# Operand tiles moved to multiples of 128 bytes, and jobs moved between the cast and the low half in a chained fp32 kernel

## The chip, the core and the metric

The kernel runs on one core of a Trainium2 chip. The metric is the time of one execution on the device in microseconds (us): before the change 1062.71 us, the median of three runs from 1061.94 to 1063.3. TensorE (PE in the profile) multiplies, VectorE (DVE) and ScalarE (ACT) do the elementwise work, SyncE (SP) issues nearly all DMAs. [...]

## The reference

Three layers, one after the other, on 6016 tokens of 256 channels:

```python
qn = q / (norm(q, axis=1) + 1e-06);  kn = k / (norm(k, axis=1) + 1e-06)
s = kn.transpose(0, 2, 1) @ qn / tau          # 256 x 256: over channels, not tokens
a = exp(s - s.max(-1));  a /= a.sum(-1) + 1e-09
x = v @ a                                     # 6016 x 256
h = x @ w_in;   x = (h * sigmoid(1.702 h)) @ w_out        # 256 -> 2048 -> 256
h = x @ w2_in;  out = maximum(0.01 h, h) @ w2_out         # 256 -> 2048 -> 256
```

The four weight matrices arrive as float64 and the result is float32.

## The kernel before

**Products.** Every float32 operand x of the two large layers is split into a high part (x rounded to the format float32r) and a low part (the rest). A product is three matmuls (`terms`, L84): high by high, high weight by low token, low weight by high token. Tokens are the moving operand, 512 columns at a time (448 in the last pair of blocks); a weight block of 128 x 128 is the stationary one and is loaded for each matmul.

**Front.** q and k are streamed through `qk` tiles and multiplied in plain float32 (L365), the squares give the norms, and the softmax gives the 256 x 256 matrix, whose halves are `eth` and `etl`. `fold(f)` (L461) multiplies it into the first layer's input weights, so that v can be used as it is.

**Layers.** There are 8 weight groups f and 6 pairs of token blocks. In the first pair of the first layer `hidden_first` (L639) makes the hidden block directly; one call per f and half s, 16 calls, and `fold(f + 1)` between them. From the second pair on, `step` (L673) makes a 2 x 2 block of products with 7 instead of 8 multiplications (sums of token blocks in `xa` and `xb`, sums of weight blocks in `wa`). Results of the activation go to `gd`, `g11` and `g22` as halves and wait in the list `pend` until `emit_y` (L504) issues their second product into the banks y00 to y11. A step is 12 matmuls with `xa`, 12 with a waiting pair of halves, 9 with `xb`, and 12 again.

**Order.** All instructions are written out by hand in each engine's order; there is no scheduler. Preparing the weights (turning float64 words to float32, splitting, forming sums) is one long generator of small jobs, `jobs` (L272); `go_on(n)` puts the next n of them where it stands. A job is mostly one DVE instruction, sometimes an ACT instruction or a DMA. `fetch` does the same for the next pair's tokens. Before the last pair of the first layer the rest of the jobs is issued at once (L754). `switch` (L621) splits the next pair's `xb`.

**Places of the tiles.** Tiles of a pool stand one after the other, each rounded up to 32 bytes per partition. `ident` takes 512 bytes and `ones` 4, so 32; all that follows in the pool `early` begins 32 bytes past a multiple of 128: `wa` and `wo` of f = 0 to 2, `xa0`, `xb`, `eth`, `etl`. Then come `den` and `rden` with 8 bytes each, and all that follows them begins 96 bytes past such a multiple: `ws`, `qk`, and in the pool `late` `xa1`, `wa` and `wo` of f = 3 to 7, `g11`, `g22`, `gd`. The layer-2 weights take the same places as the layer-1 ones. All the sizes of these operands are multiples of 128 bytes.

Of the kernel before, what the change touches and what calls it, by code (L numbers as in the profile page):

```python
# [7 lines left out]
F32 = mybir.dt.float32  # L8
# [9 lines left out]
def tile_kernel(  # L18
# [28 lines left out]
    nc = tc.nc  # L47
# [24 lines left out]
    ps = ctx.enter_context(tc.tile_pool(name="ps", bufs=1, space=bass.MemoryType.PSUM))  # L72

    ident = const.tile([P, P], F32, name="ident")
    ones = const.tile([P, 1], F32, name="ones")
    x2 = [dram.tile([P, 4, w], F32, name=f"x2{p}") for p, w in enumerate(width)]
    w1raw = [dram.tile([P, 4, P], F32, name=f"w1raw{f}") for f in range(NF)]
    w2a = [dram.tile([P, 2, 7, P], F32, name=f"w2a{f}") for f in range(NF)]
# [31 lines left out]
    with tc.manual_schedule():  # L110
# [78 lines left out]
        def convert(key):  # L189


            name, f = key
            if key not in scaled:
                scale_words(raws[key])
                scaled.add(key)
            t = raws[key]
            b = t[:, :, :, 1]
            a = early.tile([P, 4, P], I32, tag="ta", name="ta", bufs=2)
            nc.vector.tensor_scalar(  # L199
                out=a, in0=t[:, :, :, 0], scalar1=29, scalar2=7,  # L200
                op0=ALU.logical_shift_right, op1=ALU.bitwise_and,
            )
            yield
            nc.vector.scalar_tensor_tensor(  # L204
                out=a, in0=b, scalar=-0x80000000, in1=a, op0=ALU.bitwise_and, op1=ALU.bitwise_or
            )
            yield
            nc.vector.scalar_tensor_tensor(  # L208
                out=a, in0=b, scalar=3, in1=a, op0=ALU.logical_shift_left, op1=ALU.bitwise_or
            )  # L210
            raws.pop(key)
            to_convert.remove(key)
            next_load()
            scale_next()
            yield
            a = a.bitcast(F32)
            flat = a.rearrange("p k c -> p (k c)")
            if name == "wo":
                hi, lo = (wo[f][:, s].rearrange("p k c -> p (k c)") for s in range(2))
                nc.vector.tensor_copy(hi, flat)  # L220
                yield
                subtract(lo, flat, hi.bitcast(F32))
                yield
                return
            if name == "wi":
                wi = early.tile([P, 2, BLK], F32R, tag="ws", name="wi", bufs=2)
                nc.vector.tensor_copy(wi[:, 0], flat)
                yield
                subtract(wi[:, 1], flat, wi[:, 0].bitcast(F32))
                ready[f] = wi  # L230
                yield
                return
            if name == "w2o":
                w = early.tile([P, 2, BLK], F32R, tag="ws", name="w2o", bufs=2)
                nc.scalar.copy(w[:, 0], flat)
                yield
                subtract(w[:, 1], flat, w[:, 0].bitcast(F32))
                nc.sync.dma_start(
                    out=w2o[f].rearrange("p h s c -> p h (s c)"), in_=w.bitcast(F32)
                )  # L240
                yield
                return
            hi, lo = (
                early.tile([P, 7, P], F32R, tag="ws", name=f"w2a{x}", bufs=2) for x in "hl"
            )
            nc.scalar.copy(hi[:, :3], a[:, :3])
            yield
            subtract(lo[:, :3], a[:, :3], hi[:, :3].bitcast(F32))
            yield
            yield from combine(a)  # L250
            nc.scalar.copy(hi[:, 3:], a)
            yield
            subtract(lo[:, 3:], a, hi[:, 3:].bitcast(F32))
            for i, x in enumerate((hi, lo)):
                nc.sync.dma_start(out=w2a[f][:, i], in_=x.bitcast(F32))
            yield

        ready, combined = {}, set()

        def combine_first(f):  # L260

            a = early.tile([P, 4, P], F32, tag="ta", name="ts", bufs=2)
            nc.sync.dma_start(out=a, in_=w1raw[f])
            yield
            yield from combine(a)
            nc.scalar.copy(wa[f][:, 0, 3:], a)
            yield
            subtract(wa[f][:, 1, 3:], a, wa[f][:, 0, 3:].bitcast(F32))
            combined.add(f)
            yield  # L270

        def jobs():  # L272
            for key in order[:2 * NF]:
                yield from convert(key)
            for f in range(NF):
                yield from combine_first(f)
            for key in order[2 * NF:]:
                yield from convert(key)
# [8 lines left out]
        big = [front.tile([P, 2, 2, 4, C], F32, name=f"qk{i}") for i in range(4)]  # L287
        acc = front.tile([P, 2, 2, C], F32, name="acc")
        sc = front.tile([P, KC, C], F32, name="sc")
        taub = front.tile([P, 1], F32, name="taub")  # L290
        rtau = front.tile([P, 1], F32, name="rtau")
        dq = front.tile([P, KC, P], F32, name="dq")
        root = front.tile([P, 4], F32, name="root")
        rr = front.tile([P, 4], F32, name="rr")
        rn = front.tile([P, 4], F32, name="rn")
        mx = front.tile([P, KC], F32, name="mx")
        rk = front.tile([P, KC], F32, name="rk")
        st = front.tile([P, KC, C], F32, name="st")
        den = early.tile([P, KC], F32, name="den")
        rden = early.tile([P, KC], F32, name="rden")  # L300
        nc.vector.memset(acc, 0.0)


# [157 lines left out]
        def fold(f):  # L461

            wi = ready.pop(f).rearrange("p h (d n) -> p h d n", d=KC)
            pw = bank("h2").rearrange("p (k n) -> p k n", k=KC)
            for kc in range(KC):
                c0 = slice(kc * P, (kc + 1) * P)
                for d in range(KC):
                    terms(pw[:, kc], (eth[:, d, c0], etl[:, d, c0]), (wi[:, 0, d], wi[:, 1, d]),
                          d == 0, d == KC - 1)
            raw = early.tile([P, 4, P], F32, tag="tp", name="raw")  # L470
            for kc in range(KC):

                nc.scalar.activation(
                    out=raw[:, 0::3] if kc == 0 else raw[:, 1:3],
                    in_=pw[:, kc].rearrange("p (s n) -> p s n", s=2), func=AF.Copy,
                    scale=rden[:, kc:kc + 1],
                )
            hi, lo = wa[f][:, 0, :4], wa[f][:, 1, :4]
            nc.vector.tensor_copy(hi, raw)  # L479
            subtract(lo, raw, hi.bitcast(F32))  # L480
            nc.sync.dma_start(out=w1raw[f], in_=raw)
# [145 lines left out]

        def reload(f):

            pool = early if f < EARLY else late  # L630
            wa[f] = pool.tile([P, 2, 7, P], F32R, tag=f"wa{f}", name=f"wa2{f}")
            nc.sync.dma_start(out=wa[f].bitcast(F32), in_=w2a[f])

        def reload_out(f):
            pool = early if f < EARLY else late
            wo[f] = pool.tile([P, 2, 2, C], F32R, tag=f"wo{f}", name=f"wo2{f}")
            nc.sync.dma_start(out=wo[f].bitcast(F32), in_=w2o[f])

        def hidden_first(f):  # L639
# [5 lines left out]
            for u in range(2):  # L645
# [2 lines left out]
                    terms(hp, (wa[g][:, 0, at[kc]], wa[g][:, 1, at[kc]]),  # L648
                          (x[:, 0, u], x[:, 1, u]), kc == 0, kc == KC - 1)
                act(1, h[:, u], hp)  # L650
            halves(gd[:, 0], gd[:, 1], h)
            for u in range(2):
                pend.append((1, 0, u, f, gd[:, 0, u], gd[:, 1, u]))

# [5 lines left out]
        for f in range(NF):  # L660
            for s in range(2):
                hidden_first(f + s * NF)

                if f + 1 < NF and s == (f == 0):
                    while f + 1 not in ready:
                        go_on(1)
                    fold(f + 1)
                if f + 1 < NF or s == 0:
                    emit_y(len(pend) - 2)
                go_on(6)  # L670
                fetch()

        def step(layer, p, f):  # L673
# [24 lines left out]
            g22 = late.tile([P, 2, BLK], F32R, tag="gs", name="g22", bufs=3)[:, :, :w]  # L698
            act(layer, tt, tt)
            nc.scalar.copy(g22[:, 0], tt)  # L700
            second = pend[2:]
            del pend[2:]
            emit_y(2)
            go_on(2)
            fetch()
            subtract(g22[:, 1], tt, g22[:, 0].bitcast(F32))
            product(pa, A12, xbt, B21, more=True)
# [9 lines left out]
            subtract(g11[:, 1], tp, g11[:, 0].bitcast(F32))  # L717
            act(layer, cc, cc)
            pend.extend(second)
            emit_y(2)  # L720
            pend.append((layer, p, 1, f + NF, g22[:, 0], g22[:, 1]))
            pend.append((layer, p, 0, f, g11[:, 0], g11[:, 1]))
            begun.append((layer, p, f, cc))
            go_on(3)
            fetch()

        begun = []
# [1 line left out]
        def finish_step():  # L729
            if begun:  # L730
# [4 lines left out]
                pend.append((layer, p, 1, f, gd[:, 0, 0], gd[:, 1, 0]))  # L735
                pend.append((layer, p, 0, f + NF, gd[:, 0, 1], gd[:, 1, 1]))

        steps = [(layer, p) for layer in (1, 2) for p in range(NPAIR)]
        for i, (layer, p) in enumerate(steps[1:], 1):
            switch(layer, p)  # L740
            coming[0] = prefetch(*steps[i + 1]) if i + 1 < len(steps) else iter(())
            for f in range(NF):
                while f not in combined:
# [5 lines left out]
                        reload_out(f - 1)  # L749
                elif i == NPAIR and f == 0:  # L750
                    reload_out(NF - 1)
            while coming[0] and next(coming[0], 1) != 1:
                pass
            if (layer, p) == (1, NPAIR - 2):  # L754
                for _ in work:
                    pass
        finish_step()
        emit_y(len(pend))

# [29 lines left out]
```

## Time and profile before

| what | value |
|---|---|
| median of three runs | 1062.71 us |
| the profiled execution's own time | 1062.7 us |
| its span in the profile | 1060.9 us |
| TensorE busy | 1041.6 us (98%), 4664 matmuls |
| VectorE busy | 777.7 us (73%) |
| ScalarE busy | 590.2 us (56%) |
| mean granted TensorE clock | 0.996 |

The chain of work that ended last is followed back from the last instruction; 93% of it is TensorE, 48% in `y` products and 44% in `h` products. Busy time of TensorE counts a matmul from its start to its modelled end, and these overlap: one of 512 columns is listed with some 390 ns while the next one starts some 230 ns after it. How fast matmuls follow each other is read from the chain, whose pieces run from one start to the next, or from the starts in the timeline.

### The profile page before, as it was taken

The numbers are of one execution on the slowest core, as the hardware profiler recorded it, in microseconds if no ns is written. First come the engines' busy times: TensorE is split into PE (matmuls) and PEld (weight loads), VectorE is DVE, ScalarE is ACT, GpSimd is POOL, SyncE is SP. The second block draws the span as 40 slices with busy tenths as digits, with TensorE's granted clock in tenths as the row PEclk, the third lists the DMA queues.
The fourth block names the chain that finished last, engine by engine and source line by source line (L and its number), as shares of the span: only waits on it lengthen the run. The fifth ranks groups of instructions, "written<-read, shape, count | busy, mean of one in ns | idle before, by whom it ended". The sixth has DMA issues, their size and how long they took to land.

```text
span 1060.9 us, 12596 instructions
## 1 busy us (share of the span) xinstructions
PE 1041.6 (98%) x4664; PEld 867.8 (82%) x4664; DVE 777.7 (73%) x1185; ACT 590.2 (56%) x862; POOL 0.7 (0%) x7
## 2 busy tenths in 40 slices
PE   7999999999999999999999999999999999999996
PEld 6878887888888888888998888888888888888996
DVE  5979868788888888887676667667577667667654
ACT  5555546566656656565556555555555555555452
POOL 0000000000000000000000000000000000000000
PEclk9999999999999999999999999999999999999998
DMA  9645323015224324202644002101200300300202
GB/s 357 247 109 140 125 84 90 11 38 157 95 75 125 89 76 149 74 36 86 212 164 149 1 1 43 38 1 25 55 0 15 66 1 1 74 1 1 41 1 35
DMA packets 120077, 81.82 MB, mean 77 GB/s; under 512 B 93392, under 2 KB 104400, under 8 KB 118736
## 3 DMA queue, kind: packets, MB, share of 16 engines
q1 hardware_dynamic: 116160, 80.43, 25.6%
q10 hardware_dynamic: 3856, 0.59, 0.4%
q8 instruction: 36, 0.59, 0.2%
q14 instruction: 25, 0.20, 0.1%
HBM read 55.05 MB, written 25.95 MB: 76 GB/s over the span
## 4 chain that ended last, share of the span: by engine, by line
PE 93%; DVE 3%; DMA 2%; ACT 1%; issue 0%; SPq 0%; DVEq 0%; ACTq 0%
PE y L88 48%; PE h L88 44%; DVE acc L95 2%; DMA qk<-in_k_dram 1%; DMA qk<-in_q_dram 1%; SPq L316 0%; DVE gd L92 0%; ACT gd L91 0%; DVE ta L208 0%; ACT sq L332 0%; DVE ta L204 0%; ACT h L496 0%; DVE xb L92 0%; DVE o L557 0%; DVE ta L199 0%
## 5 line engine op out<-in xcount | busy, mean ns | idle before, releaser
L88 PE MATMUL y<-gd,wo 128*128 128x512 f32 (+1 forms) x1248 | 297.7, 387 | 0.0
L88 PE MATMUL h<-xa,wa 128*128 128x512 f32 (+1 forms) x1152 | 279.5, 388 | 0.3 <-DVE wa L479 0.3
L88 PEld LDWEIGHTS y<-gd,wo 128*128 128x128 f32 x1248 | 233.8, 188 | 46.7
L88 PEld LDWEIGHTS h<-xa,wa 128*128 128x128 f32 x1152 | 216.0, 188 | 44.2 <-DVE wa L479 0.5
L88 PE MATMUL y<-g,wo 128*128 128x512 f32 (+1 forms) x1056 | 250.6, 386 | 0.0
L88 PEld LDWEIGHTS y<-g,wo 128*128 128x128 f32 x1056 | 198.3, 188 | 38.2
L88 PE MATMUL h<-xb,wa 128*128 128x512 f32 (+1 forms) x888 | 221.6, 389 | 2.0 <-ACT tp L689 1.0
L88 PEld LDWEIGHTS h<-xb,wa 128*128 128x128 f32 x888 | 166.2, 187 | 37.4 <-DVE tt L95 1.6
L95 DVE TENSOR_TENSOR tv<-tp,h 128x512 f32<-128x512 f32 (+1 forms) x88 | 59.4, 675 | 123.1 <-PE h L88 119.9
L95 DVE TENSOR_TENSOR cc<-tv,h 128x512 f32<-128x512 f32 (+1 forms) x176 | 116.5, 673 | 39.7 <-PE h L88 38.6
L689 ACT COPY tp<-h 128x512 f32<-128x512 f32 (+1 forms) x88 | 50.8, 577 | 102.3 <-PE h L88 100.5
L92 DVE TENSOR_TENSOR gd<-cc,gd 128x1024 fp32r<-128x1024 f32 (+1 forms) x88 | 105.1, 1194 | 1.5 <-ACT gd L91 1.5
L91 ACT CAST gd<-cc 128x1024 fp32r<-128x1024 f32 (+1 forms) x88 | 90.9, 1033 | 0.0
L498 ACT ACTIVATE cc<-cc 128x1024 f32<-128x1024 f32 (+1 forms) x48 | 50.1, 1044 | 40.3 <-DVE cc L95 40.3
L498 ACT ACTIVATE tt<-tt 128x512 f32<-128x512 f32 (+1 forms) x48 | 30.0, 625 | 72.9 <-DVE tt L95 72.9
L95 DVE TENSOR_TENSOR tt<-tt,h 128x512 f32<-128x512 f32 (+1 forms) x88 | 59.4, 675 | 9.9 <-DVE tt L95 0.9
L95 DVE TENSOR_TENSOR tt<-tv,h 128x512 f32<-128x512 f32 (+1 forms) x88 | 59.4, 676 | 9.2
L95 DVE TENSOR_TENSOR g<-tt,g 128x512 fp32r<-128x512 f32 (+1 forms) x88 | 59.1, 672 | 8.2 <-ACT g L700 8.0
L496 ACT ACTIVATE cc<-cc 128x1024 f32<-128x1024 f32 (+1 forms) x40 | 41.6, 1041 | 38.0 <-DVE cc L95 38.0
L496 ACT ACTIVATE tt<-tt 128x512 f32<-128x512 f32 (+1 forms) x40 | 24.9, 623 | 63.6 <-DVE tt L95 63.6
L95 DVE TENSOR_TENSOR g<-tp,g 128x512 fp32r<-128x512 f32 (+1 forms) x88 | 59.1, 672 | 0.0
L700 ACT CAST g<-tt 128x512 fp32r<-128x512 f32 (+1 forms) x88 | 53.8, 611 | 2.8
(85 smaller groups left out, 699.4 us busy)
## 6 DMA issues: line engine op xcount, KB each, us to landing
cv<-in_moe_w_in_dram SPq DMA_DIRECT2D x32, 256.0 KB, 3.2
cv<-in_moe_w_out_dram SPq DMA_DIRECT2D x16, 512.0 KB, 3.7
wa<-w2a SPq DMA_DIRECT2D x8, 896.0 KB, 4.6
qk<-in_q_dram SPq DMA_DIRECT2D x10, 512.0 KB, 8.7
qk<-in_k_dram SPq DMA_DIRECT2D x10, 512.0 KB, 9.1
x<-stg SPq DMA_DIRECT2D x5, 1024.0 KB, 4.4
stg<-x SPq DMA_DIRECT2D x5, 1024.0 KB, 5.5
out_dram<-o SPq DMA_DIRECT2D x80, 64.0 KB, 2.0
```

Of the source, the lines that this page charges most:

```text
L88: nc.tensor.matmul(dst, lhsT=w, rhs=x, start=start, stop=stop, skip_group_check=more)
L91: nc.scalar.copy(hi, raw)
L92: nc.vector.tensor_tensor(out=lo, in0=raw, in1=hi.bitcast(F32), op=ALU.subtract)
L95: nc.vector.tensor_tensor(out=out, in0=in0, in1=in1, op=op)
L496: nc.scalar.activation(out=out, in_=in_, func=AF.Gelu_apprx_sigmoid)
L498: nc.scalar.activation(out=out, in_=in_, func=AF.Prelu, alpha=0.01)
L689: nc.scalar.copy(tp, pa)
L700: nc.scalar.copy(g22[:, 0], tt)
```

## The change

It has four parts.

1. Small tiles (`ones`, `taub`, `rtau`, `root`, `rr`, `rn`, `mx`, `rk`, `den`, `rden`) take 128 bytes per partition, of which the old part is used. All operands of products then begin at a multiple of 128 bytes. No product instruction changes otherwise.
2. In `hidden_first` four of the six jobs stand between the cast of the high half and the subtraction that makes the low half, instead of all six behind `emit_y`. The last call has none.
3. `fold(1)` stands ahead of the cast in the ninth call and uses bank h0; later folds use h3 instead of h2. At the end of the first pair its next-to-last products are issued before the first step's, and a step issues half of what waits.
4. `switch` for the second pair stands directly behind the first pair, and jobs left over are issued when `reload` needs them; the weights that `combine_first` reads back are loaded one ahead.

```diff
-    ones = const.tile([P, 1], F32, name="ones")
+    def small(pool, n, name):
+        return pool.tile([P, 32], F32, name=name)[:, :n]
+    ones = small(const, 1, "ones")
...
+        def load_first(f):
+            if f < NF:
+                a = early.tile([P, 4, P], F32, tag="ta", name="ts", bufs=2)
+                nc.sync.dma_start(out=a, in_=w1raw[f])
+                first_weights[f] = a
...
-            a = early.tile([P, 4, P], F32, tag="ta", name="ts", bufs=2)
-            nc.sync.dma_start(out=a, in_=w1raw[f])
-            yield
+            a = first_weights.pop(f)
+            load_first(f + 1)
...
-        den = early.tile([P, KC], F32, name="den")
-        rden = early.tile([P, KC], F32, name="rden")
+        den = small(early, KC, "den")
+        rden = small(early, KC, "rden")
...
-            pw = bank("h2").rearrange("p (k n) -> p k n", k=KC)
+            pw = bank("h0" if f == 1 else "h3").rearrange("p (k n) -> p k n", k=KC)
...
+            while ("w2i", f) not in stored:
+                go_on(1)
...
-            halves(gd[:, 0], gd[:, 1], h)
+            if f == NF:
+                fold(1)
+            nc.scalar.copy(gd[:, 0], h)
+            if f < 2 * NF - 1:
+                go_on(4)
+            subtract(gd[:, 1], h, gd[:, 0].bitcast(F32))
...
+                emit_y(len(pend) - 2)
                 if f + 1 < NF or s == 0:
-                    emit_y(len(pend) - 2)
-                go_on(6)
+                    go_on(2)
                 fetch()
...
-            second = pend[2:]
-            del pend[2:]
-            emit_y(2)
-            go_on(2)
+            half = len(pend) // 2
+            second = pend[half:]
+            del pend[half:]
+            emit_y(half)
+            if f:
+                go_on(2)
...
-            go_on(3)
+            if f < NF - 1:
+                go_on(3)
...
+        switch(1, 1)
         for i, (layer, p) in enumerate(steps[1:], 1):
-            switch(layer, p)
...
-            if (layer, p) == (1, NPAIR - 2):
-                for _ in work:
-                    pass
+            if i + 1 < len(steps):
+                switch(*steps[i + 1])
```

ScalarE in the second call of `hidden_first` and at `fold(1)` (`h2_500` is the hidden block in bank h2, `raw` the folded weights), before:

```order
L178 ACTIVATE cv_352<-cv_352 128x512
L496 ACTIVATE h_498<-h2_500 128x512
L496 ACTIVATE h_498<-h3_508 128x512
L91 CAST gd_499<-h_498 128x1024
L473 ACTIVATE raw_531<-h2_518,rden_134 128x2x128
```

The same place after the change:

```order
L182 ACTIVATE cv_352<-cv_352 128x512
L510 ACTIVATE h_498<-h2_500 128x512
L510 ACTIVATE h_498<-h3_508 128x512
L487 ACTIVATE raw_529<-h0_516,rden_134 128x2x128
L487 ACTIVATE raw_529<-h0_516,rden_134 128x256
L671 CAST gd_499<-h_498 128x1024
```

The folded product moves from bank h2, which ScalarE reads just before it, to h0, which was read one call earlier, and the cast of `gd` now stands behind it.

VectorE from the last two calls of the first pair to the first step (`ts` and `wa<-ts` are jobs, `xb` the halves for the second pair, `tv` and `tt` the step's sums), before:

```order
L92 TENSOR_TENSOR gd<-h,gd 128x1024
L95 TENSOR_TENSOR ts<-ts 128x128 x3
L95 TENSOR_TENSOR wa_451<-ts,wa_451 128x512
L92 TENSOR_TENSOR xb<-stg,xb 128x512 x3
L95 TENSOR_TENSOR tv<-tp,h_1296 128x512
```

After:

```order
L99 TENSOR_TENSOR ts<-ts 128x128 x3
L99 TENSOR_TENSOR gd<-h,gd 128x1024
L99 TENSOR_TENSOR ts<-ts 128x128
L99 TENSOR_TENSOR gd<-h,gd 128x1024
L96 TENSOR_TENSOR xb<-stg,xb 128x512 x3
L99 TENSOR_TENSOR tv<-tp,h_1307 128x512
```

The four job instructions between the last `gd` and `xb` are gone from there.

TensorE at the same place, before:

```order
L88 MATMUL h_1272<-xb,wa_459 128x512 x3
L88 MATMUL h_1295<-xa_450,wa_103 128x512 x3
L88 MATMUL h_1296<-xa_450,wa_103 128x512 x3
L88 MATMUL h_1297<-xa_450,wa_103 128x512 x3
L88 MATMUL h_1298<-xa_450,wa_103 128x512 x3
L88 MATMUL y_537<-gd,wo_460 128x512 x3
L88 MATMUL y_538<-gd,wo_460 128x512 x3
L88 MATMUL y_545<-gd,wo_460 128x512 x3
L88 MATMUL y_546<-gd,wo_460 128x512 x3
L88 MATMUL h_1295<-xb,wa_103 128x512 x3
```

After:

```order
L92 MATMUL y_554<-gd,wo_460 128x512 x3
L92 MATMUL y_555<-gd,wo_460 128x512 x3
L92 MATMUL h_1306<-xa_450,wa_103 128x512 x3
L92 MATMUL h_1307<-xa_450,wa_103 128x512 x3
L92 MATMUL h_1308<-xa_450,wa_103 128x512 x3
L92 MATMUL h_1309<-xa_450,wa_103 128x512 x3
L92 MATMUL y_546<-gd,wo_460 128x512 x3
L92 MATMUL y_547<-gd,wo_460 128x512 x3
L92 MATMUL h_1306<-xb,wa_103 128x512 x3
```

Twelve `y` matmuls now stand ahead of the step's `xa` products, and six instead of twelve between these and the `xb` products.

## Rows read from the trace of the kernel before

**Rows 1.** The page, busy time: us, share of the span, instructions.

```profile
PE 1041.6 (98%) x4664; PEld 867.8 (82%) x4664; DVE 777.7 (73%) x1185; ACT 590.2 (56%) x862; POOL 0.7 (0%) x7
```

**Rows 2.** Stretches: us, busy time (instructions) by engine, PEclk, DMA share, GB/s.

```profile
300.00:400.00 100.00, 100.00 (x437) 81.82 (x437) 85.67 (x138) 62.27 (x94) 0.00 (x0) 1.00 0.32 97
...
600.00:700.00 100.00, 100.00 (x436) 81.65 (x436) 67.23 (x95) 53.46 (x77) 0.00 (x0) 1.00 0.11 22
```

**Rows 3.** Groups by form, matmuls of the products: count, busy us and mean ns, idle.

```profile
L88 PE MATMUL y<-gd,wo 128*128 128x512 f32 x1056 | 256.4, 391 | 0.0
L88 PE MATMUL h<-xa,wa 128*128 128x512 f32 x960 | 238.1, 392 | 0.3 <-DVE wa L479 0.3
L88 PE MATMUL y<-g,wo 128*128 128x512 f32 x864 | 209.2, 391 | 0.0
L88 PE MATMUL h<-xb,wa 128*128 128x512 f32 x744 | 189.9, 394 | 2.0 <-ACT tp L689 1.0 <-DVE tt L95 0.9
...
L88 PE MATMUL h<-xa,wa 128*128 128x448 f32 x192 | 41.4, 364 | 0.0
L88 PE MATMUL y<-gd,wo 128*128 128x448 f32 x192 | 41.4, 364 | 0.0
L88 PE MATMUL y<-g,wo 128*128 128x448 f32 x192 | 41.3, 364 | 0.0
L88 PE MATMUL h<-xb,wa 128*128 128x448 f32 x144 | 31.7, 364 | 0.0
```

**Rows 4.** The chain in order of time, second layer: start us, us, what.

```profile
604.63 2.74 PE y L88 x12
...
615.01 2.74 PE y L88 x12
...
632.97 2.80 PE h L88 x12
...
646.10 2.72 PE y L88 x12
...
650.87 2.76 PE y L88 x12
653.63 2.75 PE h L88 x12
...
661.18 2.76 PE y L88 x12
```

**Rows 5.** The chain in the last pair, matmuls of 448 columns.

```profile
1038.42 2.43 PE h L88 x12
```

**Rows 6.** Timeline of PE in the first fold: start us, us, instruction.

```profile
56.81 0.41 PE L88 MATMUL h<-wi,etl 128*128 128x256 f32 x1
...
57.45 0.41 PE L88 MATMUL h<-wi,etl 128*128 128x256 f32 x1
```

**Rows 7.** Timeline of PE in the second fold.

```profile
67.22 0.28 PE L88 MATMUL h<-wi,etl 128*128 128x256 f32 x1
...
67.57 0.28 PE L88 MATMUL h<-wi,etl 128*128 128x256 f32 x1
```

**Rows 8.** Stretches of the two folds, columns as in rows 2.

```profile
55.90:57.60 1.70, 1.70 (x10) 1.70 (x9) 0.86 (x2) 0.30 (x1) 0.00 (x0) 0.50 0.72 242
66.90:68.00 1.10, 1.10 (x11) 1.10 (x11) 1.03 (x3) 0.89 (x1) 0.00 (x0) 1.00 0.00 0
```

**Rows 9.** Timeline of PE in the front, plain float32 products.

```profile
38.71 2.11 PE L365 MATMUL y<-qk 128*128 128x256 f32 x9
```

**Rows 10.** Waits of PE from 55 us on: us in total, times, longest us.

```profile
PE h L88 <- ACT tp L689: 1.0, 1, 1.0
PE h L88 <- ACT h L496: 1.0, 1, 1.0
PE h L88 <- DVE tt L95: 0.9, 1, 0.9
```

**Rows 11.** Timeline of DVE, the last low half of the first pair.

```profile
155.99 1.23 DVE L92 TENSOR_TENSOR gd<-h,gd 128x1024 fp32r<-128x1024 f32 x1 [2.21 <-ACT gd L91]
```

More of the change, by code (lines that the diff above doesn't have):

```diff
@@ L240, in convert @@
                 )
+                stored.add(key)
                 yield
@@ L255, in convert @@
                 nc.sync.dma_start(out=w2a[f][:, i], in_=x.bitcast(F32))
+            stored.add(key)
             yield
-        ready, combined = {}, set()
+        ready, combined, stored = {}, set(), set()
+        first_weights = {}
+        def load_first(f):
[3 more added lines that the diff above has]
+                first_weights[f] = a
         def combine_first(f):
-            a = early.tile([P, 4, P], F32, tag="ta", name="ts", bufs=2)
-            nc.sync.dma_start(out=a, in_=w1raw[f])
-            yield
+            a = first_weights.pop(f)
+            load_first(f + 1)
             yield from combine(a)
@@ L274, in jobs @@
                 yield from convert(key)
+            load_first(0)
             for f in range(NF):
@@ L289, in tile_kernel @@
         sc = front.tile([P, KC, C], F32, name="sc")
-        taub = front.tile([P, 1], F32, name="taub")
-        rtau = front.tile([P, 1], F32, name="rtau")
+        taub = small(front, 1, "taub")
+        rtau = small(front, 1, "rtau")
         dq = front.tile([P, KC, P], F32, name="dq")
[L293 to L297, printed above, removed]
+        root = small(front, 4, "root")
+        rr = small(front, 4, "rr")
+        rn = small(front, 4, "rn")
+        mx = small(front, KC, "mx")
+        rk = small(front, KC, "rk")
         st = front.tile([P, KC, C], F32, name="st")
-        den = early.tile([P, KC], F32, name="den")
-        rden = early.tile([P, KC], F32, name="rden")
+        den = small(early, KC, "den")
+        rden = small(early, KC, "rden")
         nc.vector.memset(acc, 0.0)
@@ L634, in reload_out @@
         def reload_out(f):
+            while ("w2o", f) not in stored:
+                go_on(1)
             pool = early if f < EARLY else late
@@ L662, in tile_kernel @@
                 hidden_first(f + s * NF)
-                if f + 1 < NF and s == (f == 0):
+                if f + 1 < NF and s == 0:
                     while f + 1 not in ready:
                         go_on(1)
-                    fold(f + 1)
+                    if f:
+                        fold(f + 1)
+                emit_y(len(pend) - 2)
                 if f + 1 < NF or s == 0:
-                    emit_y(len(pend) - 2)
-                go_on(6)
+                    go_on(2)
                 fetch()
@@ L700, in step @@
             nc.scalar.copy(g22[:, 0], tt)
-            second = pend[2:]
-            del pend[2:]
-            emit_y(2)
-            go_on(2)
+            half = len(pend) // 2
+            second = pend[half:]
+            del pend[half:]
+            emit_y(half)
+            if f:
+                go_on(2)
             fetch()
@@ L719, in step @@
             pend.extend(second)
-            emit_y(2)
+            emit_y(half)
             pend.append((layer, p, 1, f + NF, g22[:, 0], g22[:, 1]))
@@ L751, in tile_kernel @@
                     reload_out(NF - 1)
-            while coming[0] and next(coming[0], 1) != 1:
+            for _ in coming[0]:
                 pass
-            if (layer, p) == (1, NPAIR - 2):
-                for _ in work:
-                    pass
+            if i + 1 < len(steps):
+                switch(*steps[i + 1])
         finish_step()
```

## The prediction

> **What bounds the kernel now.** I read the busy times first, then stretches of the span, the waits of TensorE, and last the chain in order of time. TensorE is busy 98% of the span [rows 1], and 100% of every stretch in the middle at full clock [rows 2]. VectorE, the next engine, is busy 85.7 of 100 us in the stretch where the layer-2 weights are prepared and 67 later [rows 2]. So the end is set by how fast TensorE's matmuls follow each other, plus its few waits, plus a front and a tail that the change hardly touches. After 55 us TensorE waits in only three places that matter, 1.0, 1.0 and 0.9 us [rows 10]. Whatever the moved jobs do for TensorE, they can't give back more than these 3 us.
>
> That leaves the rate. There are 1056 + 960 + 864 + 744 = 3624 product matmuls of 512 columns and 3 x 192 + 144 = 720 of 448 [rows 3]. The listed 391 ns is no rate, since matmuls overlap. The chain gives it. A step holds 45 matmuls and lasts 615.01 - 604.63 = 10.38 us or 661.18 - 650.87 = 10.31 us [rows 4]: 230.7 and 229.1 ns each, mean 229.9 ns. In the last pair it is 2.43 us for 12 [rows 5], 202.5 ns. [...]
>
> **What the places do.** I work out for each group how far past a multiple of 128 bytes its operands begin, from the order and sizes of the tiles (told with the kernel). At 632.97 us the moving `xa0` stands at 32 and the weights of f = 7 at 96: 2.80 us for 12, 233.3 ns. At 653.63 us `xa1` stands at 96 and the weights of f = 1 at 32: 2.75 us, 229.2 ns. At 646.10 us `g` and the output weights of f = 7 both stand at 96: 2.72 us, 226.7 ns [rows 4]. The instructions differ in nothing else that sets a rate. So the places matter, and equal ones are best. [...]
>
> [...]
>
> [...]
>
> **The change part by part.** The sum is made against the profiled execution's 1062.7 us, which is the median of the runs.
>
> Small tiles to 128 bytes. Every product operand then begins at 0. No product row of the trace has that, so bounds: from below the columns alone, 213.3 and 186.7 ns, as in the first fold; from above the slowest pair seen, 233.3 ns. I take columns and the 2.6 ns left over in the float32 products: 216.0 and 189.3 ns. [...]
> - 512 columns: 3624 x (229.9 - 216.0) = 50.4 us.
> - 448 columns: 720 x (202.5 - 189.3) = 9.5 us.
> - The folds: 96 matmuls, at most 117 - 109 = 8 ns each, 0.8 us; I count nothing.
>
> `fold(1)` in bank h0 and ahead of the cast: it waited 1.0 us for ScalarE to read h2 [rows 10]; h0 was read a call earlier. The second product behind it needs the low half of the first call, which stands three to four jobs later on VectorE, but VectorE idles there before the subtraction. 1.0 us.
>
> Second pair's halves ahead of jobs: the `xb` products waited 1.0 us for the copy `tp`, which stood on ScalarE behind three casts and a job's cast, and 0.9 us for `tt`, which stood on VectorE behind four job instructions [rows 10]. The jobs are gone from there, and TensorE has 12 + 12 + 6 matmuls between the last hidden block and `xb`, instead of 24. 1.9 us.
>
> Four jobs ahead of the low half, sixteen calls less one. Cost: the products wait for the low half if VectorE is late. Before the last subtraction of the pair it idled 2.21 us for the cast [rows 11], about four jobs. So they fit a gap. But with TensorE 6% faster VectorE rises from 85.7% to about 91% in the stretch at 300 us, and the same share holds in the first pair. From nothing to 6 us of new waits; I take 2.
>
> Jobs no longer issued in a block before the last pair, weights loaded one ahead, stores before reloads: TensorE idles at none of these now, so nothing is gained. A reload on SP now can wait for a store just issued, with later DMAs queued behind it; the reloaded weights are needed a whole pair later, some 75 us. Nothing.
>
> Sum: 50.4 + 9.5 + 2.9 - 2.0 = 60.8; 1062.7 - 60.8 = 1001.9, say 1002 us.
>
> **The rivals.**
> [...]
> - *Only the difference between the two operands counts.* Weights are loaded while the previous matmul streams. If the two reads disturb each other by their relative place, 0 and 0 is no better than 96 and 96: 226.7 and 200.0 ns. 3624 x 3.2 = 11.6, 720 x 2.5 = 1.8, waits 2.9: 16.3 us, 1046 us. For it: equal places are best. [...]
> [...]
> - *Slower: equal places collide.* Operands of TensorE, ScalarE and VectorE now all begin at 0, and if streams that begin together want the same part of the memory together, each product matmul pays as the worst pair does now, 233.3 ns: 3624 x 3.4 = 12.3 us more, less 2.9: 1072 us. It outweighs the waits from 230.7 ns per matmul on. For it: operands that differ by 64 do disturb each other by 7 ns. Against: equal ones were the fastest.
>
> **How the numbers follow.** Forecast 0.50; half 0.13; relative place 0.25; no effect 0.05; collision 0.07. Time: 1002 us. The range takes in the first three and is cut at both ends: from columns alone, 1062.7 - 60.2 - 11.4 - 2.9 = 988, to relative place with some waits, 1049. Within 0.2%, 2.1 us, no difference can be told. "No effect" at 1060 lies about there: 0.03 of it faster, 0.02 the same. Slower is the collision, a little of it fast enough for no change: 0.06, and 0.03 the same in all. Faster 0.91.
>
> **What would show it.** In the chain, 12 product matmuls take 2.59 us whatever the operands, and 2.27 us at 448 columns; steps last 9.72 us; the second fold's three take 0.33 us or less. [...] The three waits in rows 10 are gone, and no VectorE wait over 1 us stands in the first pair. VectorE is busy some 91 of 100 us around 300 us. The forecast is wrong if chains of equal place stay at 2.72 us, or if TensorE's waits on VectorE exceed 6 us.

## The result and the profile after

The changed kernel takes 1046.95 us (median of five runs, 1045.85 to 1047.54) beside 1063.3 us of the kernel before: ratio 0.9848, interval 0.9833 to 0.9862. By that ratio it is 16.2 us less, between the medians 16.35. The forecast was 1002 us, 61 us less. The direction was right; the gain is a quarter of what was forecast.

The chain in order of time, second layer, the kernel after (start us, us, what); it answers to [rows 4]:

```profile
605.01 2.72 PE y L92 x12
...
615.21 2.72 PE y L92 x12
...
632.89 2.72 PE h L92 x12
...
645.81 2.72 PE y L92 x12
...
650.57 2.72 PE y L92 x12
653.29 2.72 PE h L92 x12
```

Twelve matmuls take 2.72 us whatever their operands: 226.7 ns each. The pieces of 2.80, 2.76 and 2.75 us are gone, but the best piece of before was 2.72 us already, and none is shorter now. A step is 10.20 us where it was 10.31 to 10.38. The forecast for these rows was 2.59 us and 9.72 us.

The chain in the last pair (448 columns), after:

```profile
1023.75 2.43 PE h L92 x12
```

The same pair in the kernel before, but with one of the first three weight groups:

```profile
983.89 2.40 PE h L88 x12
...
992.92 2.40 PE h L88 x12
```

The second fold, after:

```profile
65.58 0.28 PE L92 MATMUL h<-wi,etl 128*128 128x256 f32 x1
...
65.94 0.28 PE L92 MATMUL h<-wi,etl 128*128 128x256 f32 x1
```

The last pair runs at 2.43 us for 12 as in [rows 5]; 2.27 were forecast. But [rows 5] shows the later weight groups only. With the first three, before, such pieces took 2.40 us and a step 9.03 us (from 983.89 to 992.92 us), and now they take 2.43 and 9.12: in three steps of each layer the change lost some 0.5 us. The fold has become slower, (65.94 - 65.58)/3 = 120 ns beside 117 [rows 7].

The waits of PE from 55 us on, after, and the stretch at 300 us (columns as in rows 2):

```profile
PE h L92 <- DVE etl L99: 0.2, 1, 0.2
```

```profile
300.00:400.00 100.00, 100.00 (x443) 82.81 (x442) 84.14 (x134) 62.86 (x94) 0.00 (x0) 1.00 0.31 94
```

All three waits of [rows 10] are gone; the 0.2 us that are left lie in the first fold. VectorE stands at 84% there, not at the 91% that were worked out for a TensorE 6% faster.

The profiled spans differ by 1060.9 - 1045.0 = 15.9 us. Of that 3624 x (229.9 - 226.7) = 11.6 us is the rate of 512 columns. The three waits, counted from start to start of the matmuls about them, are some 3.7 us. The 448 columns take back some 0.5 us. Some 1.2 us lies behind the last product (from 1051.8 to 1060.9 before, from 1037.1 to 1045.0 after), where the last outputs land; in the runs below this tail took 7.7 to 9.2 us with no pattern, so I give it to no part of the change. The four make 16.0 us.

### The profile page after: what moved, and what is told of

The parts are those of the page before. It is cut to its first block, busy times and chain, and to the rows that moved or that the text cites. A ratio compares the mean times of both kernels' runs of the same rounds, so it can differ in the third digit from the quotient of the medians.

```text
span 1045.0 us, 12600 instructions
## 1 busy us (share of the span) xinstructions
PE 1031.1 (99%) x4664; PEld 870.1 (83%) x4664; DVE 774.5 (74%) x1185; ACT 590.0 (56%) x862; POOL 0.7 (0%) x7
## 4 chain that ended last, share of the span: by engine, by line
PE 93%; DVE 3%; DMA 2%; ACT 1%; SPq 1%; issue 0%; DVEq 0%; ACTq 0%
PE y L92 49%; PE h L92 44%; DVE acc L99 1%; DMA cv<-in_moe_w_in_dram 1%; DMA qk<-in_k_dram 1%; DMA ts<-w1raw 1%; SPq L330 0%; DVE ta L212 0%; DVE gd L99 0%; ACT sq L346 0%; DVE ta L208 0%; PE y L406 0%; ACT cv L182 0%; DVE o L571 0%; ACT gd L671 0%
## 5 line engine op out<-in xcount | busy, mean ns | idle before, releaser
L92 PE MATMUL h<-xa,wa 128*128 128x512 f32 (+1 forms) x1152 | 276.4, 385 | 0.0
L92 PE MATMUL h<-xb,wa 128*128 128x512 f32 (+1 forms) x888 | 217.4, 385 | 0.0
L737 ACT CAST g<-tp 128x512 fp32r<-128x512 f32 (+1 forms) x88 | 53.8, 611 | 2.8
```

Source lines behind the costliest of these rows:

```text
L92: nc.tensor.matmul(dst, lhsT=w, rhs=x, start=start, stop=stop, skip_group_check=more)
L737: nc.scalar.copy(g11[:, 0], tp)
```

## The experiments

The first theory after the result was the rival of the relative place: only the place of the two operands of a matmul relative to each other counts.

**The two halves of the change apart.** The first run takes the kernel before with the small tiles alone:

```diff
-    ones = const.tile([P, 1], F32, name="ones")
+
+    def small(pool, n, name):
+        return pool.tile([P, 32], F32, name=name)[:, :n]
+
+    ones = small(const, 1, "ones")
...
-        den = early.tile([P, KC], F32, name="den")
+        den = small(early, KC, "den")
...
```

> The kernel before with the small tiles alone at 128 bytes, the order of the work untouched. Relative place (the theory after the result): all product operands are equal modulo 128, so matmuls of 512 columns go from 229.9 to 226.7 ns as in the changed kernel, 3624 x 3.2 = 11.6 us, and the three waits of 2.9 us stay: about 1051.5 us. Rival, the gain is in the order: 1060 or more, with chain pieces that still differ.

The second takes the changed kernel with their old sizes:

```diff
-        return pool.tile([P, 32], F32, name=name)[:, :n]
+        return pool.tile([P, n], F32, name=name)
```

> The changed kernel with the small tiles at their old sizes, so the new order alone with the old places. Relative place: only the waits go, 1063.3 - 2.9 to 4 = about 1060 us, and chain pieces of 2.72 to 2.80 us for 12 come back. Rival, the order carries the gain: about 1050 us.

Measured: places alone 1052.78 us beside 1063.38, ratio 0.9901 (0.9886 to 0.9916), by which it is 10.5 us; order alone 1058.94 us, 0.9959 (0.9947 to 0.9972), 4.4 us. Together 14.9 of 16.2 us, so the parts add up within their intervals. With places alone the chain pieces are 2.72 us; with order alone those of 2.80 and 2.74 us are back. The places run lies 1.3 us above its expectation. There the wait at the second pair's halves is still in the program, and behind it the clock falls. Stretches of the places run (columns as in rows 2):

```profile
155.00:160.00 5.00, 3.86 (x17) 2.58 (x15) 4.25 (x9) 2.66 (x5) 0.00 (x0) 1.00 0.14 23
160.00:165.00 5.00, 4.09 (x12) 3.22 (x12) 3.94 (x9) 2.38 (x5) 0.00 (x0) 0.66 0.01 3
165.00:170.00 5.00, 5.00 (x24) 4.13 (x23) 3.61 (x7) 4.18 (x6) 0.00 (x0) 1.00 0.34 134
```

The third number from the end, PEclk, is 0.66 in the middle row, after TensorE had stood idle for about 2 us in two pieces, 1.1 us and, in this row, 0.9; the first six matmuls behind them took 2.93 us, 488 ns each. In this row 12 matmuls were started, where 5 us at 226.7 ns hold 22. The kernel before has the same two waits, and in its profiled execution the clock stayed at 1.00 behind them:

```profile
160.00:165.00 5.00, 3.27 (x13) 2.22 (x14) 3.94 (x9) 2.26 (x5) 0.00 (x0) 1.00 0.00 0
```

From 155 to 165 us it started 34 matmuls, the places run 29: some 1.1 us, about what the places run lies above its expectation. All four runs of it have a mean granted clock of 0.994, those of the kernel before beside it 0.996 to 0.998. Why the clock fell in the one and not in the other is not shown. In the changed kernel the stretch is idle nowhere and the clock stays at 1.00.

**All operands at 32.**

```diff
     ones = small(const, 1, "ones")
+    const.tile([P, 8], F32, name="gap")
```

> The changed kernel with one more tile of 32 bytes ahead of the others, so every product operand begins 32 bytes past a multiple of 128. Relative place: the same 1047 us, 12 matmuls in 2.72 us. Rival, multiples of 128 are what counts: 33 columns' worth or more per matmul back, between 1051 and 1063 us.

Measured 1048.0 us, 0.9858 (0.9845 to 0.9872) of before, beside 0.9848: no difference that can be told, and 2.72 us for 12. So multiples of 128 bytes are not what counts: operands that begin at 32 or at 0 run alike.

**The rate by itself.** Two operand tiles in SBUF, sliced at chosen places, 24 matmuls per place:

```diff
+                nc.tensor.matmul(
+                    t[:c, :n], lhsT=wts[:, wo:wo + c], rhs=mov[:, mo:mo + n],
+                    start=True, stop=True,
+                )
```

> Matmuls alone, 24 in a row per setting, nothing of the reference's computation; two operand tiles, sliced at places 0, 32, 64, 96 and finer. Relative place: the spacing depends on the difference of the two places alone, 226.7 ns when equal, 229 and 233 ns when 64 apart. [...]

The chain in order of time; the tile's name says the place, m for the moving operand, w for the weights, a to d for 0, 32, 64 and 96, and the last three are weights at 256 and weight blocks of 64 and 32 columns:

```profile
20.87 5.45 PE mawa L37 x24
...
31.91 5.60 PE mawc L37 x24
...
48.72 5.45 PE mbwb L37 x24
...
65.36 5.51 PE mcwa L37 x24
...
104.19 5.44 PE mdwd L37 x24
...
126.40 5.44 PE wtwofiftysix L37 x24
...
165.04 5.52 PE chalf L37 x24
170.56 5.56 PE cquarter L37 x24
```

Equal places give 5.44 to 5.45 us, 226.7 ns, at 0, 32 and 96 alike. With the moving operand at 0 and the weights at 64 it is 5.60 us, 233 ns, and the other way round 5.51 us, 229 to 230 ns: the two numbers of [rows 4]. So the sign of the difference counts too. Narrower weights are no faster (230 and 232 ns), so the weight block's bytes don't set the time. Fewer moving columns at equal places gave 206 ns for 448, 173.3 for 384 and 120 for 256, and 512 columns of bfloat16 gave 216. From 512 to 256 columns 106.7 ns go, 0.417 ns a column. By this estimate 512 columns alone are some 213 ns, and some 13 ns of the 226.7 are left over; below they are called the surplus. It is not the same for all widths: for 448 the estimate makes 200.0 ns with it, and 206 were measured.

**More places.**

> Matmuls alone again, nothing of the reference's computation: the moving operand 4 to 252 bytes past a multiple of 256, weights at 0, 16 in a row per place; then 448 and 256 columns in steps of 16 bytes; then a moving operand of every second element. [...] The strided operand, if blocks of 128 bytes set the rate: about twice 226.7 ns; if elements do: 226.7 ns.

Chain: moving operand at 0, 64, 128, 132 and 252 past the weights with 512 columns, 16 matmuls each; 448 columns at 0 and 32; 256 at 0, 64 and 112; every second element:

```profile
21.13 3.63 PE maax L37 x16
...
80.48 3.66 PE mcax L37 x16
...
139.98 3.73 PE meax L37 x16
143.71 3.83 PE mebx L37 x16
...
255.79 3.64 PE mhhx L37 x16
259.43 3.25 PE pax L37 x16
...
265.92 3.20 PE pcx L37 x16
...
311.45 1.92 PE qax L37 x16
...
319.04 1.88 PE qex L37 x16
...
324.74 1.84 PE qhx L37 x16
...
341.70 7.26 PE stride L55 x16
```

None of 64 places is under 3.63 us, 226.7 ns. It is not reached at equal places alone; 28, 60, 108, 236 and 240 bytes apart give 3.63 us too. At 128 apart it is 3.73 us (233 ns); in the run before, weights 256 and 512 bytes on gave 5.44 us for 24, 226.7 ns, again, so what equal places give comes back at 256 bytes and not at 128. And 448 and 256 columns are not fastest at equal places: 200 instead of 203 ns at 32, and 115 instead of 120 ns at 112. For 256 columns runs differ: with the weights 64 past the moving operand it was 114 ns in the run before and 118 in the run of types below. The fold's moving operand stood 64 past its weights before the change (96 and 32): 117.5 ns here, 117 in [rows 7], and 120 at equal places. That is why it lost by the change. The strided operand takes 7.26 us, 454 ns a matmul, twice as long: the columns alone do not set the time. What does, the run of types below takes up.

**Places turned against the whole kernel.** Gaps of 64 bytes ahead of the layers' weights and behind them, and in the second run of 128 (`[P, 32]`):

```diff
+        early.tile([P, 16], F32, name="gap0")
         for f in range(EARLY):
             weights(early, f)
+        early.tile([P, 16], F32, name="gap1")
         xa[0] = early.tile([P, 2, 4, BLK], F32R, name="xa0")
...
         xa[1] = late.tile([P, 2, 4, BLK], F32R, name="xa1")
+        late.tile([P, 16], F32, name="gap2")
         for f in range(EARLY, NF):
             weights(late, f)
+        late.tile([P, 16], F32, name="gap3")
```

> The changed kernel with gaps of 64 bytes, so that all weights of the layers stand 64 bytes past the moving operands' places; order and computation as in the changed kernel. Relative place: 233.5 ns for each of 3624 matmuls as in the row of single settings, 6.8 ns more, 24.6 us: about 1072 us, slower than the kernel before. [...]

> The changed kernel with gaps of 128 bytes instead of 64, so that every product operand still lies at a multiple of 128, but all weights of the layers 128 bytes past a multiple of 256 and the moving operands at one. If multiples of 128 are the condition: 1047 us and 2.72 us for 12. If the period is 256, as the single settings say (233.4 ns at 128 apart, 226.7 at 256): spacing between 230 and 233 ns, 1059 to 1071 us.

Measured: 64 apart 1061.1 us, 0.998 of before (0.997 to 0.9989); 128 apart 1068.71 us, 1.0045 (1.0028 to 1.0062). The chain of the first and then of the second, second layer:

```profile
622.84 2.75 PE y L92 x12
...
630.43 2.79 PE h L92 x12
...
640.81 2.75 PE h L92 x12
...
653.89 2.80 PE y L92 x12
```

```profile
622.54 2.78 PE y L92 x12
625.32 2.79 PE h L92 x12
```

The second kernel holds every product operand at a multiple of 128 bytes, as the change says, and is slower than the kernel before. So the change's own aim is not what made it faster. Its operands are equal modulo 256 only because `den` and `rden`, which stand between the two groups of places, are two tiles of 128 bytes; an odd number of them would have put many of the products 128 apart, as in this run. Nothing in the change provides for that.

The first kernel took 231 ns a matmul (10.38 us for a step of 45), not the 233.5 of its expectation, which was 11 us too high. The expectation had the edit wrong: not all weights stand 64 past. By the order of the tiles, those of f = 3 to 7 stand 64 past `xa` and `xb`, but 64 ahead of `gd`, `g11` and `g22`, which lie behind the last gap; for f = 0 to 2 it is the other way round. The chain shows it: late in a pair `h` takes 2.79 us and `y` 2.75; with the next pair's first groups, from 640.81 us on, it is `h` 2.75 and `y` 2.80. These are the two numbers of the single settings, 229 to 230 and 233 ns, and about half of the matmuls have either. Their mean, 231.4 ns, makes an estimate of 1064 us, 3 us above the measured 1061.1.

**The four jobs.** The changed kernel with the jobs behind the low half:

```diff
             nc.scalar.copy(gd[:, 0], h)
+            subtract(gd[:, 1], h, gd[:, 0].bitcast(F32))
             if f < 2 * NF - 1:
                 go_on(4)
-            subtract(gd[:, 1], h, gd[:, 0].bitcast(F32))
```

> The changed kernel with the four jobs behind the low half again. The gain of the order came from fold(1) and from the second pair's halves, so this part is worth nothing: 1047 us, within 0.2%. Rival: the jobs in VectorE's gap are what keeps TensorE from waiting at the faster rate: waits on VectorE in the first pair and 1049 to 1053 us.

Measured 1050.58 us, 0.9887 (0.987 to 0.9903), beside 0.9848 (0.9833 to 0.9862) of the changed kernel: some 3.5 us slower, the rival's size. Its waits of PE from 55 us on:

```profile
PE h L92 <- DVE tt L99: 1.1, 1, 1.1
PE h L92 <- DVE eth L464: 0.8, 1, 0.8
PE h L92 <- DVE wi L231: 0.7, 1, 0.7
PE h L92 <- DVE wi L99: 0.3, 1, 0.3
```

`fold(1)` now waits for `wi`, which stands on VectorE behind a subtraction that itself waits for the cast, and the second pair's `xb` products wait for `tt` again. The wait for `eth` is the first fold's and not the jobs' doing: the changed kernel, profiled once more, has it too (0.8 us). From places alone to the changed kernel it was 5.8 us between the medians, so more than half of what the order gives there hangs on the jobs standing in the gap.

**What the surplus is.** Moving operands of every element, every second and every fourth, in three types:

> Matmuls alone, 24 in a row per setting, nothing of the reference's computation: float32r, bfloat16 and plain float32, with moving operands of every element, every second and every fourth, and float32r of 480 and 320 columns. Theory: the surplus is a limit on the bytes that the moving operand's read passes over, about 9.04 per ns and partition (2048 bytes in 226.7 ns), with the strided float32r row of 451 ns as its mark. [...]

Chain: r is float32r, b bfloat16, f plain float32 (two records per matmul); one, two and four the step; `bfour` has 256 columns, `neight` 480 and `nthree` 320 of float32r, the others 512:

```profile
20.77 5.44 PE rone L46 x24
26.21 10.87 PE rtwo L46 x24
37.08 11.07 PE rfour L46 x24
...
59.27 5.19 PE bone L46 x24
64.47 5.42 PE btwo L46 x24
69.89 5.44 PE bfour L46 x24
75.33 20.60 PE fone L46 x48
95.93 21.60 PE ftwo L46 x48
117.53 43.20 PE ffour L46 x48
160.73 5.22 PE neight L37 x24
165.95 3.52 PE nthree L37 x24
```

Bfloat16 takes 216 ns (5.19/24) and with every second element, 4 bytes per column, 226 ns; 256 columns of 8 bytes each take 227 ns. Plain float32 goes from 429 to 450 and 900 ns a record. In these rows 9.0 to 9.1 bytes are passed over per ns and partition: 2048 in 226 to 227 ns, 4096 in 450, 8192 in 900. A surplus that is fixed for each float32r matmul and absent elsewhere is refuted: bfloat16 did not stay at 216 ns, and 256 columns of float32r had a place with 115 ns, where the 13 ns over the columns would make 120.

But the rate is not shown to be the whole cause either. float32r of every fourth element took 461 ns, where 8192 bytes at that rate would make some 900. And at equal places the shorter widths lie above the rate: 480 columns took 217 ns and 320 took 147, where 2048 bytes in 226.7 ns would make 212.5 and 141.7. A rate fits the 512 columns and the strides of the other two types; what the 13 ns of float32r are stays open.

**The last pair at its own place.** 448 columns leave 256 bytes of a tile free, so the halves can begin 64 bytes in:

```diff
+    def cols(w):
+        o = 0 if w == BLK else 16
+        return slice(o, o + w)
...
-                terms(dst, (wf[:, 0, a], wf[:, 1, a]), (xs[:, 0, b, :w], xs[:, 1, b, :w]),
+                terms(dst, (wf[:, 0, a], wf[:, 1, a]), (xs[:, 0, b, cols(w)], xs[:, 1, b, cols(w)]),
```

> The changed kernel, but in the last pair of blocks (448 columns in tiles of 512) the halves begin 64 bytes into their tiles. Matmuls of 448 columns took 200.0 ns with the moving operand 64 past the weights and 202.7 ns in the changed kernel; 720 x 2.7 = 1.9 us less: 1045 us. If the place doesn't carry over to the whole kernel: no difference from the changed kernel.

> The changed kernel itself once more, on the chip and in the rounds of the other three, for comparison with the run of the last pair: 1047 us by every theory.

Measured in the same rounds: 1044.91 us, 0.9825 of before (0.9811 to 0.984), beside 1047.22 us, 0.9844 (0.983 to 0.9859), of the changed kernel. The chain of the first in the last pair:

```profile
1022.86 2.40 PE h L96 x12
```

2.40 instead of 2.43 us for 12, 200 ns, in 720 matmuls 1.8 us of the 2.3 between the medians. The intervals overlap, so the time alone would not prove it, but the chain does. It is the fastest of all versions here.

## Why the prediction was wrong

- **The step that failed** is the term "small tiles to 128 bytes", where I took "columns and the 2.6 ns left over in the float32 products: 216.0 and 189.3 ns". It was put at 50.4 + 9.5 us and measured 226.7 and 202.5 ns: 11.6 us won and some 0.5 us lost. No run shows 216.0 and 189.3 ns for float32r, nor the bound of 213.3 and 186.7 ns for the columns alone. The bound was my estimate, the first fold's 213 ns for 256 columns at a granted clock of 0.50 [rows 6, 8], halved for a clock of 1.00; the 2.6 ns are about what the float32 products' 216 ns lie above it. In their place the runs showed 226.7 ns at best for 512 columns, and 200.0 to 202.7 for 448 in the whole kernel. The upper part of the surplus, 3.2 ns, was a matter of places; the lower 13 ns stayed, and at 512 columns none of 64 places takes it away. The float32 products took (2.11 - 0.38)/8 = 216 ns a record of 256 columns [rows 9], with 0.38 us estimated for the last one: 0.84 ns a column, where the layers' matmuls took 0.45 (229.9/512). So they could not say what places do at nearly twice the rate. What the 13 ns are is open: a limit on the bytes read fits 512 columns and not the shorter ones.
- The evidence was there and I read it halfway. 2.72 us appeared for a pair that was equal, both operands at 96, not for a pair that was aligned [rows 4]. That a multiple of 128 bytes brings more than equal places do was an estimate of mine; no row showed it, and the fold's matmuls, with operands at 96 and 32, were faster before (117 ns [rows 7]) than aligned (120). That the surplus belongs to reading operands is not shown either. What is measured: the first fold's matmuls took 213 ns at a granted clock of 0.50, less than twice the 117 ns of the second at 1.00 [rows 6 to 8], and bfloat16 went from 216 to 226 ns when it passed over as many bytes as float32r.
- "Only the difference between the two operands counts" was the rival at 0.25, with 1046 us; 1046.95 came. Its price for 512 columns, 11.6 us, is what the trace shows. That the relative place counts, and not the multiple of 128, is shown by the runs at 32 and at 64 and 128 apart; its reason, that the two reads disturb each other, is not. Its 226.7 ns is also the lowest of the 64 places. For 448 columns its 200.0 ns, an estimate, was wrong: equal places give 202.7 there. So its closeness is in part luck: 1.8 us that it won there were some 0.5 lost, while the waits gave 3.7 instead of 2.9 and 1.2 lie in the tail.
- That 448 columns take 202.5 ns before was read from the later weight groups alone; with the first three, the chain has 2.40 us for 12, 200.0 ns.
- "Half", with half of the surplus left, was held at 0.13: none of 64 places had a 512-column matmul under 226.7 ns. "No effect" was held at 0.05. The runs with equal and shifted weights differ by 22 us (1047 to 1069 us): places cost time here.
- The waits: `fold(1)` and the second pair's halves gave what was counted, 2.9 us listed and 3.7 from start to start. The four jobs were booked as 2 us lost; no wait shows that they lose anything, and the run with them behind is 3.5 us slower. The sign was wrong: I asked whether they fit the gap, not who waits for the jobs themselves.
- Jobs no longer in a block, weights one ahead, stores before reloads: no wait stands at any of them after. That they are worth nothing was not tested apart.
- The collision of equal places did not occur: at 512 columns no place was faster than equal ones.

## What to carry to other kernels

Before giving a surplus per instruction to one cause, look for the best case that the trace holds: the best row, not the ideal, is what an alignment can be expected to reach, unless a row shows more. A step that no row shows gets half the chance, not the point forecast. For float32r streams like these, put moving operands and weights at equal places modulo 256 bytes when 512 columns are streamed (226.7 ns, beside 233 at 128 apart), and measure places apart for other widths (448 columns took 200 ns at 32 apart and 203 at equal places). A multiple of 128 bytes for every tile is not enough: that kernel took 1068.71 us.

## What the hardware showed that was not expected

- A 512-column float32r matmul with its weights loaded each time takes 226.7 ns at best, over 64 places (mean granted clock of that run 0.970; in the run of 24 per place, with the same 226.7 ns, it was 1.00 in every stretch up to 200 us). Bfloat16 took 216 ns in a stream of its own, and 226 ns with 4 bytes per column.
- The relative place of the moving operand and the weights costs up to 13 ns at 512 columns (3.84 us for 16 matmuls, 240 ns, at 196 and 244 bytes apart, 3.83 at 132, beside 3.63), and with weights 256 and 512 bytes on the time of equal places is back (5.44 us for 24). Why, no run here shows.
